# Attention, dense layer and soft mixture of experts on one core: output stores of two column parts on the copying engine's queue, with a new order and new engines

## The chip, the cores and the metric

The kernel runs on one core of a Trainium2 chip. The core has TensorE (PE; its weight loads are listed as PEld), VectorE (DVE), ScalarE (ACT), GpSimd (POOL) and SyncE (SP), each with its own queue of instructions that it works off in order. Transfers run on 16 DMA engines; an instruction on one of the engines' queues, mostly SP's, starts each of them. The metric is the device time of one execution in microseconds (us).

## The reference

```python
def reference(**kwargs):          # B, H, S, D = 4, 8, 576, 64
    attn_out = _attn_ref(...)     # rotary embedding of q and k, softmax(q k^T / 8) v
    x = attn_out.transpose(0, 2, 1, 3).reshape(B * S, H * D)   # 2304 tokens x 512
    h = x @ w_in                  # 512 -> 2048
    x = (np.maximum(h, 0) + alpha * np.minimum(h, 0)) @ w_out  # 2048 -> 512
    logits = x @ phi              # 8 experts of 4 slots: 32 columns
    d = softmax over the tokens of logits; slot_input = d.T @ x          # 32 x 512
    for e in range(8):            # 512 -> 1024 -> 512 for its 4 slots
        slot_out[e] = np.maximum(slot_input[e] @ w1[e], 0) @ w2[e]
    c = softmax over the slots of logits
    return c @ slot_out           # 2304 x 512, float32
```

## The kernel before, in words

**One list of operations.** The kernel does not issue instructions as it goes. Every step is an operation (`op`) with an engine, a cost, the operations it needs and the buffers that it takes and uses. Where a step can run on several engines, `choose` reads one digit of the table `ENGINES` (794 digits) and so picks ScalarE, VectorE or GpSimd. `Plan.order` then decodes the table `ORDER`, a full sequence of all 2791 operations, and the last loop of the kernel issues them in that sequence. What stands in an engine's queue, and in which order, is thus set by the two tables alone. A transfer stands in SP's queue, unless its line names another engine.

**The front.** Per pair of heads, q and k are loaded, rotated (L338 to L449) and multiplied on TensorE to scores `st` (L480, L489 to L493). VectorE takes each row's maximum (L498), ScalarE the exponential with its row sum (L503, tile `e`), and the rows are normalised on ScalarE (L225), VectorE (L227) or GpSimd (L229, helper `times`). Batch 0's pieces are transposed on TensorE (`pt` L578, `pc` L628); those of the other batches on VectorE (L565, L598) and by way of DRAM (`sc` L607, `ET` L617, `ett` L615). L662 multiplies by the values (`pv`). `top` (L245) transposes a per-column maximum for the scales of the weights.

**The middle.** The dense layer runs block by block: `ph` (L839) is x @ w_in; the leaky step is a product `rl` on ScalarE (L850) or VectorE (L852, chosen) and a sum `g` on VectorE (L857). w_out is not applied to the tokens: it is folded with phi for the logits (L881), and the slots collect the tokens' sums in front of w_out (L1033, L1044).

**The late loads.** When the last `pv` is done, the attention's memory becomes a pool of 29 buffers (class x). From there SP loads w_out in 16 transfers of 512 KB (`wor`, L1191) and the experts' weights in 65 transfers of 256 KB to 1 MB (`xw`, L1246); the latter use, beside the x buffers, those that the dense layer gives up. Each `wor` is turned into two TensorE operands by three steps on VectorE (`wo`, L1199, L1201, L1203), behind which its buffer is free. `px` (L1308) is the slots' sums times w_out and needs all 16.

**The end.** `expert_in` (L1365 with `relu` and transposes `pth` L1391) and `expert_out` (`po`, L1426) are the experts. The output has 512 columns, worked on in three parts of 256, 128 and 128: `PARTS = ((0, 0, 256), (1, 256, 128), (1, 384, 128))`. Per part VectorE makes `mov` of `po` (L1447, L1452). `final(ph, n)` then multiplies the tokens' weights `est` by `mov` (`pf`, L1548) for the token tiles of `n`, copies the result to `ob` on VectorE (L1553) or ScalarE (L1555, chosen), and issues the store (L1563; L1566 for the tiles 16 and 17, in two halves). In the third part a store of L1563 goes out by ScalarE's queue if ScalarE made the copy; all others of L1563 by SP's.

Of the kernel before, what the change touches and what calls it, by code (L numbers as in the profile page):

```python
# [34 lines left out]
ENGINES = (  # L35
    "020000000210000102000000000010101110101000001010201010102000100200020200102011100100000110020210111020010020001000010001"
    "002000102000010200000202010000100000000200000202000000000000200012000000002020010000000202201000001001000000222100000000"
    "200000020001021000200022000200000200001120020000000200202000200002002211210010020000202000000002000201201000220020000002"
    "022000202002002000201000101010000202000010002002210011000100000200002000002002002200000110001000202202000202000012000021"
    "000020000000020000000002210201221001120100202220000000002002000120020000000200002000202000002000200001120010000000000010"  # L40
    "000021100000110000000110201001100010010010012000000010010000001111010100000010010001200010001000001000100100000011111110"
    "00002010000101000001100000100000100011000100010001000001011110100001010111"
)


ORDER = (
    "c-"
    "mc72|!J0`#;Y)cWGZxR4Nrko5qqxMZ;)O(qhfXU_P=9X8iw#7#U<4n#nTFFrPt)EG0uV(P$;4MT!&^HI=2sy|?Awd*1K7?>V<Jr`tL2@;txi_x#?K5(DHgEYJYsAJGgb2e*mT#?WavvK"
    "GJ=9$It(*c1<unEzw`5A;rh8i42aV3$)rLeC8{18NIBp{;c&fMIp3cfE~qnOFVbS~nTgjM6WUKHLrW#&%bS*UUU?0gdjm(cS<*cf=fMnpkW!w3;>VX|D~?gPKy&=kj4KGB2Z!pXZBS+N"
    "xgJo?YBv)?pHISZQVSYh-QH%k{0Vni|%^`|}>oy;6|&R<OFpW}fjdym35CKH>rQK80eR948aF<J3|Q;8`*Pbl^cih1{%i;*bhv<n1h9Q<v=NjqudO^0lS)%3~$Npx(OK>~v`7XfT9)Q4"  # L50
    "0(<{xGGrsZD-0(y3DhmgQg$V*#K9^y^;^ol*{Za&6iin%Ksm8&<AqHdgs8?cO18bQlTpOCim#W;IBg-MIfj4WoKZrLVP2@<$D0noXg#%kBZ#!7~$m%K{jyFnwVMwIkDf%3yf*^z0!Epx"
    "UCTYPMWd1tN(>+wew(y+NU8Q=MnWjd9SPx#I~K2GwsgUTm8-"
    "d)Xg<&Pw%c>g*8f76j<DBpuVKkbPSB&HvYfLv1)*9K*f}ez9pjV{c<ow&_r@{qyng&8aNixdq^C=vD?$`m4w6v@c)1d^$I6tZnkTZf44tHhxFG{`F)IyvT!<Qx|{xBz>yNse0l*(Jc0+"
    "zh$#Sv)_e<32TzqCso>f<pVLzp0i31a$0o^g{e9jKW68R&jarxpOkJkyzbo<_DxxKhQW45$?T$_$-*U15tgD8{Mlc0L5xo1@7tR!Jp7`}x8|lDN-"
    "c#6WvUC$HyXc#!?5A{i_8rXr=%gCWzoA19IxG;1UsK4)yVXliXszWzbG*N)YA2tA&kApZt2dwu;m)S(f@n6^|ifg2taDE_;R^hzF`b}8@JID<}3}r8{2ie9V$H$T?)1pNVZ?A>!DA3Uf"
# [106 lines left out]
def attn_moe_softmoe(ctx, tc, qx, kx, vx, w_in, w_out, alpha, phi, w1, w2, tab, msks, w_out_t, out):  # L162
    nc = tc.nc
# [50 lines left out]
    PE, ACT, DVE, POOL, DMA = "PE", "ACT", "DVE", "POOL", "DMA"  # L214
# [475 lines left out]
    PF = FF // NPC  # L690
# [3 lines left out]
    sw = cst.tile([128, NPC], F32, name="sw")  # L694
# [428 lines left out]
    n = 0  # L1123
# [21 lines left out]
    for b in range(B):  # L1145
        r = 64 * (b % 2)
# [173 lines left out]
    m = None  # L1320
# [204 lines left out]
    def final(ph, n):  # L1525
# [10 lines left out]
        for i, its in enumerate(pieces):  # L1536
# [135 lines left out]
```

## Time and profile before

| | us |
|---|---|
| three runs | 555.9, 558.49, 560.74 |
| median | 558.49 |
| the profiled execution | 558.93 |
| its span in the trace | 557.1 |

How to read it: the trace is of one execution, and its times count from the start of the span, so a sum of edits is made against the profiled execution. The windows cut the span into stretches; each row has start and end, length, then busy time and number of instructions of PE, PEld, DVE, ACT and POOL, the clock that TensorE was granted (1.00 is 2.4 GHz, 0.50 is 1.2 GHz), the busy share of the 16 DMA engines, and GB/s. The timeline has start, duration, engine, line, operation, output tile and inputs, shape and count; in brackets the idle time before it and what ended it. "SPq" and "ACTq" are the issuing of transfers on SP's and ScalarE's queue. A group of instructions has its line, engine, operation, tiles, shapes and count, then busy us in all and mean ns of one, then the idle time before and what ended it.

### The profile page before, as it was taken

The page shows a single profiled execution, that of the slowest core. Times are in us where ns is not written, and L with a number is a line of the kernel's source. Part 1 is how long each engine was busy: PE and PEld are TensorE (multiplying, and loading weights), DVE is VectorE, ACT ScalarE, POOL GpSimd, SP SyncE. Part 2 cuts the span into 40 slices and gives each one's busy share as a digit, 9 for nine tenths or more (in the row PEclk, how much of TensorE's full clock was granted, in tenths as well). Part 3 has the DMA queues.
Part 4 walks back from the last instruction along what each step waited for, and adds up shares of the span by engine and source line. Part 5 has one row for each costly group of instructions (what it writes and reads, how often), then busy time and mean ns, then how long its engine had stood idle before and what let it go on. Part 6 is the DMA issues. An engine that isn't in the chain of part 4 may idle for free.

```text
span 557.1 us, 14738 instructions
## 1 busy us (share of the span) xinstructions
PE 528.2 (95%) x5752; PEld 393.6 (71%) x5752; DVE 476.0 (85%) x1092; ACT 332.6 (60%) x805; POOL 270.8 (49%) x259
## 2 busy tenths in 40 slices
PE   2899999999999998999999999999999999999994
PEld 1454566678878787787877688877778878854573
DVE  4998999999999998999999889999876999863641
ACT  3799999997778675597666477884531122330141
POOL 2474776488898876689584588642000000001000
PEclk9998999999999999999999999999999999999997
DMA  8982855918899998898987789798774999899989
GB/s 300 392 310 92 308 162 156 294 57 281 271 355 300 309 298 274 255 330 268 342 305 241 263 307 342 258 310 308 242 238 146 412 406 396 289 366 385 405 296 271
DMA packets 80805, 160.74 MB, mean 289 GB/s; under 512 B 5344, under 2 KB 44640, under 8 KB 80736
## 3 DMA queue, kind: packets, MB, share of 16 engines
q1 hardware_dynamic: 79792, 159.18, 82.7%
q8 instruction: 45, 0.74, 0.5%
q10 hardware_dynamic: 944, 0.62, 0.4%
q14 instruction: 24, 0.20, 0.1%
HBM read 115.75 MB, written 36.96 MB: 274 GB/s over the span
## 4 chain that ended last, share of the span: by engine, by line
PE 82%; DMA 8%; DVE 6%; ACT 2%; issue 1%; SPq 1%; POOL 0%; DVEq 0%
PE ph L839 33%; PE pv L662 14%; PE st L493 9%; PE pu L1033 3%; PE lg L881 3%; PE st L480 3%; PE po L1426 2%; PE pt L578 2%; DMA wraw<-in_moe_w_in_dram 2%; DMA xw<-in_moe_w_dram 2%; DMA ET<-sc 2%; PE ph L1365 2%; PE pf L1548 1%; PE st L489 1%; DVE mm L498 1%; PE st L491 1%
## 5 line engine op out<-in xcount | busy, mean ns | idle before, releaser
L839 PE MATMUL ph<-xt,w 128*128 128x256 f16 x1536 | 182.6, 273 | 0.0
L839 PEld LDWEIGHTS <-w 128*128 128x128 f16 x1728 | 162.3, 98 | 28.8 <-issue 6.5
L503 ACT ACTIVATE e<-st,mm 128x576 f32<-128x576 f32 x144 | 106.2, 738 | 47.2 <-DVE mm L498 41.1
L498 DVE TENSOR_REDUCE mm<-st 128x1 f32<-128x576 f32 x144 | 105.9, 742 | 8.0 <-PE st L493 5.0
L229 POOL TENSOR_SCALAR e<-e,mm 128x576 f32<-128x576 f32 (+1 forms) x76 | 59.4, 787 | 72.3 <-DVE mm L529 65.4
L372 POOL TENSOR_TENSOR xn<-xn,tabs 128x576 f32<-128x576 f32 x52 | 78.6, 1525 | 11.5 <-issue 5.5
L850 ACT ACTIVATE rl<-ph 128x256 f32<-128x256 f32 x105 | 38.8, 378 | 69.4 <-PE ph L839 66.7
L662 PE MATMUL pv<-ET,vt 128*64 128x256 f32 (+1 forms) x640 | 77.0, 385 | 1.7 <-DMA ET<-sc 1.5
L565 DVE STREAM_TRANSPOSE tb<-e 128x512 f32<-128x512 f32 (+1 forms) x108 | 75.7, 706 | 2.4 <-POOL e L229 1.2
L493 PE MATMUL st<-ks,qs 128*128 128x288 f32 x384 | 73.6, 315 | 0.5 <-issue 0.5
L857 DVE SCALAR_TENSOR_TENSOR g<-rl,oma,ph 128x256 f32<-128x256 f32 x144 | 66.2, 466 | 8.6 <-ACT rl L850 7.5
L662 PEld LDWEIGHTS pv<-ET,vt 128*64 128x64 f32 (+1 forms) x640 | 42.8, 137 | 28.0 <-issue 7.4
L493 PEld LDWEIGHTS st<-ks,qs 128*128 128x128 f32 x384 | 54.3, 189 | 4.9 <-issue 2.6
L225 ACT ACTIVATE e<-e,mm 128x576 f32<-128x576 f32 (+1 forms) x72 | 51.6, 723 | 7.5 <-DVE mm L529 7.0
L873 DVE STREAM_TRANSPOSE gb<-g 128x512 f32<-128x512 f32 x64 | 43.5, 690 | 0.2
L397 POOL TENSOR_TENSOR qs<-xn,qs 64x576 fp32r<-64x576 f32 x23 | 33.8, 1468 | 15.4 <-ACT qs L219 13.0
L480 PE MATMUL st<-ks 64*128 64x288 f32 (+1 forms) x168 | 30.8, 468 | 10.2 <-DVE ks L343 7.2
L375 POOL TENSOR_TENSOR xn<-xn 128x576 f32<-128x576 f32 x24 | 35.4, 1477 | 7.4 <-DVE xn L372 6.2
L480 PEld LDWEIGHTS st<-ks 64*128 64x128 f32 (+1 forms) x168 | 17.5, 195 | 19.4 <-DVE ks L343 7.2
L503 ACT ACTIVATION_READ_ACCUMULATOR e<-st,mm 128x1 f32 x144 | 28.3, 197 | 0.0
L229 POOL TENSOR_SCALAR edt<-edt,vb 128x256 f32<-128x256 f32 x5 | 2.4, 478 | 48.0 <-ACT edt L979 47.9
L578 PE MATMUL pt<-idf,e 128*128 128x128 f32 x144 | 23.4, 292 | 2.3 <-ACT e L225 1.0
(198 smaller groups left out, 805.9 us busy)
## 6 DMA issues: line engine op xcount, KB each, us to landing
sc<-tb SPq DMA_DIRECT2D x48, 576.0 KB, 4.8
ET<-sc SPq DMA_DIRECT2D x24, 1152.0 KB, 7.6
xw<-in_moe_w_dram SPq DMA_DIRECT2D x42, 512.0 KB, 8.9
xn<-in_k_dram SPq DMA_DIRECT2D x15, 576.0 KB, 6.3
xn<-in_q_dram SPq DMA_DIRECT2D x15, 576.0 KB, 5.1
wraw<-in_moe_w_in_dram SPq DMA_DIRECT2D x8, 1024.0 KB, 9.9
wraw<-in_w_out_t_dram SPq DMA_DIRECT2D x8, 1024.0 KB, 5.3
wor<-in_moe_w_out_dram SPq DMA_DIRECT2D x16, 512.0 KB, 9.5
```

Of the source, the lines that this page charges most:

```text
L225: nc.scalar.activation(dst, src, AF.Copy, scale=scale)
L229: nc.gpsimd.tensor_scalar(dst, src, scale, 1.0, ALU.mult, ALU.mult)
L372: engines[on].tensor_tensor(e["x"][:, w], e["x"][:, w], tabs[:, w], ALU.mult)
L480: nc.tensor.matmul(st[to, j, at:at + w], x, k[rows, z:z + w], start=True, stop=True)
L493: nc.tensor.matmul(st[:, j, 0:288], r["q"][:, 768 * h + 128 * s:768 * h + 128 * s + 128].bitcast(F32R), r["k"][:, a, h, ks].bitcast(F32R), ...
L498: nc.vector.tensor_reduce(c["mm"][:, h:h + 1], c["st", h][:, :, 0:288], axis=AX.XY, op=ALU.max, negate=True)
L503: nc.scalar.activation(c["e"][:, h].rearrange("p (a n) -> p a n", a=2), c["st", h][:, :, 0:288], AF.Exp, bias=c["mm"][:, h:h + 1], accum_o ...
L565: nc.vector.transpose(out=to if tail else to[:, :, 0:8].rearrange("p q (m h) j -> p q m h j", h=2)[:, :, :, h], in_=e.rearrange("p (m q j) ...
L662: nc.tensor.matmul(pv[r], v[k, 4 * h + i if i < 4 else 8 + (h if b else 0)], x, start=(i == 0), stop=(i == 4))
L839: nc.tensor.matmul(ph, wi[j][:, wp, kc, 128 * fo:128 * fo + 128], xt[:, xp, kc, :], start=(n == 0), stop=(n == 3 * KC - 1),)
L857: nc.vector.scalar_tensor_tensor(blk["g", j][:, fo, :], c["r"], oma[:, f:f + 1], c["ph"], ALU.mult, ALU.add)
L873: nc.vector.transpose(out=blk["gt", j // 2][:, f % 8 - 1:f % 8 + 1, :].rearrange("p c n -> p (c n)"), in_=blk["g", j][:, fo - 1:fo + 1, :] ...
```

## The change

One line of code says which queue a store of L1563 uses: ScalarE's, if ScalarE made the copy, now in the second and third part. The tables `ENGINES` and `ORDER` are new. Of the 794 digits 250 differ; the counts of the three digits go from 547, 134 and 113 to 563, 113 and 118. The digits behind the normalisation of `e` move 24 from ScalarE to GpSimd, 23 back, 8 from VectorE to GpSimd and 4 in other ways; those behind `rl` move 33 from VectorE to ScalarE and 21 back. In the order an operation's place moves by 9 in the median. `ORDER` has one line more, so the changed kernel's lines are one higher behind it.

```diff
 ENGINES = (
-    "020000000210000102000000000010101110101000001010201010102000100200020200102011100100000110020210111020010020001000010001"
+    "000000000200020002000000101010101010101000000010000000202000000200021201112001111010000010020201111020110120001000010001"
...
             def store(hh, i=i, its=its, on=on):
                 k = len(its)
-                queue = nc.scalar if on == ACT and ph == 2 else nc.sync
+                queue = nc.scalar if on == ACT and ph > 0 else nc.sync
                 ob = c["ob", i].rearrange("p (k d) -> p k d", k=k)
                 if len(n) == 4:
                     to = S * (n[0] // 4) + 128 * per * i
                     queue.dma_start(out[to:to + 128 * k, cols].rearrange("(r p) d -> p r d", r=k), ob)
                     return
```

The end of ScalarE's queue, from the last turned weights `est` on; `ob` is a piece of the output, and a store of 128x4x128 is one of the second or third part, one of 64x2x128 half of the tiles 16 and 17. Before:

```order
L219 ACTIVATE est<-pe 128x384 x4
L1555 ACTIVATE ob<-pf 128x512 x4
L219 ACTIVATE est<-pe 128x384
L1555 ACTIVATE ob<-pf 128x512 x5
L1555 ACTIVATE ob<-pf 128x256
L1566 DMA out_dram<-ob 64x2x128
L1555 ACTIVATE ob<-pf 128x512
L1563 DMA out_dram<-ob 128x4x128
```

After:

```order
L220 ACTIVATE est<-pe 128x384 x2
L1556 ACTIVATE ob<-pf 128x512 x2
L1556 ACTIVATE ob<-pf 128x256
L1564 DMA out_dram<-ob 128x4x128
L1556 ACTIVATE ob<-pf 128x512 x3
L1564 DMA out_dram<-ob 128x4x128 x2
L1556 ACTIVATE ob<-pf 128x512 x2
L1567 DMA out_dram<-ob 64x2x128
L1564 DMA out_dram<-ob 128x4x128 x2
```

Four stores more stand on ScalarE, and SP's stores at the end become 16 of 20. The copy of tiles 16 and 17 in the third part is VectorE's now, and ScalarE copies more of the pieces of four.

The front of TensorE's queue: `st` scores, `pt` and `pc` transposes of the exponentials, `top` that of a maximum, `rest` the first of the weights' products. Before:

```order
L480 MATMUL st<-ks 128x288 x8
L578 MATMUL pt<-idf,e 128x128 x4
L245 MATMUL top<-idf,mws 128x128
L628 MATMUL pc<-idf,e 128x128
L480 MATMUL st<-ks 128x288 x4
L578 MATMUL pt<-idf,e 128x128 x4
L285 MATMUL rest<-w_173,dg 128x512
```

After:

```order
L481 MATMUL st<-ks 128x288 x8
L246 MATMUL top<-idf,mws 128x128
L579 MATMUL pt<-idf,e 128x128 x4
L629 MATMUL pc<-idf,e 128x128
L579 MATMUL pt<-idf,e 128x128 x4
L481 MATMUL st<-ks 128x288 x4
L286 MATMUL rest<-w_172,dg 128x512
```

`top` goes ahead of the first transposes, and the second transposes ahead of the third scores.

SP's queue where the late loads begin: `wor` is w_out, `xw` experts' weights, 128x1024 is 512 KB. Before:

```order
L1191 DMA wor<-in_moe_w_out_dram 128x1024 x10
L1246 DMA xw<-in_moe_w_dram 128x1024 x2
L1191 DMA wor<-in_moe_w_out_dram 128x1024
L1246 DMA xw<-in_moe_w_dram 128x1024 x2
L1191 DMA wor<-in_moe_w_out_dram 128x1024 x2
L1246 DMA xw<-in_moe_w_dram 128x1024
L1246 DMA xw<-in_moe_w_dram 128x512
L1246 DMA xw<-in_moe_w_dram 128x1024 x3
L1191 DMA wor<-in_moe_w_out_dram 128x1024 x2
L1246 DMA xw<-in_moe_w_dram 128x512
L1246 DMA xw<-in_moe_w_dram 128x1024
L1191 DMA wor<-in_moe_w_out_dram 128x1024
```

After:

```order
L1247 DMA xw<-in_moe_w_dram 128x512
L1192 DMA wor<-in_moe_w_out_dram 128x1024 x10
L1247 DMA xw<-in_moe_w_dram 128x512
L1192 DMA wor<-in_moe_w_out_dram 128x1024
L253 DMA msk<-in_masks_dram 128x1
L1192 DMA wor<-in_moe_w_out_dram 128x1024
L1247 DMA xw<-in_moe_w_dram 128x1024
L1192 DMA wor<-in_moe_w_out_dram 128x1024 x3
L1247 DMA xw<-in_moe_w_dram 128x1024 x14
L1192 DMA wor<-in_moe_w_out_dram 128x1024
L1247 DMA xw<-in_moe_w_dram 128x1024 x2
```

The eleventh to fifteenth load of w_out stand further ahead, and the sixteenth behind fourteen loads of experts' weights that follow on each other.

## Rows read from the trace of the kernel before

**Rows 1.** Head of the page.

```profile
span 557.1 us, 14738 instructions
```

**Rows 2.** Windows by stage: busy PE, PEld, DVE, ACT, POOL; clock; DMA share; GB/s.

```profile
0.00:50.00 50.00, 35.22 (x165) 20.06 (x165) 40.93 (x83) 35.59 (x77) 26.43 (x29) 0.97 0.82 299
50.00:110.00 60.00, 58.62 (x472) 36.13 (x470) 56.75 (x107) 57.46 (x134) 36.75 (x27) 1.00 0.65 209
110.00:425.00 315.00, 312.11 (x3554) 249.90 (x3557) 290.95 (x681) 211.31 (x525) 204.49 (x198) 1.00 0.83 274
425.00:500.00 75.00, 74.54 (x900) 58.58 (x888) 63.70 (x142) 18.30 (x52) 1.20 (x4) 1.00 0.96 369
500.00:550.00 50.00, 47.72 (x676) 28.92 (x676) 23.14 (x82) 9.95 (x21) 1.90 (x2) 1.00 0.96 352
550.00:557.10 7.10, 0.00 (x0) 0.00 (x0) 0.55 (x1) 0.00 (x0) 0.00 (x0) 0.51 0.84 228
```

**Rows 3.** Timeline of the end: issues of SP and ACT, and the last copies.

```profile
540.38 3.75 SPq L1563 DMA_DIRECT2D out_dram<-ob  x5
...
548.46 2.09 DVE L1553 COPY ob<-pf 128x512 f32<-128x512 f32 x3 [1.04 <-PE pf L1548]
548.50 0.70 ACTq L1566 DMA_DIRECT2D out_dram<-ob  x1
...
551.35 2.10 SPq L1563 DMA_DIRECT2D out_dram<-ob  x2
```

**Rows 4.** Windows of the end, columns as in rows 2.

```profile
536.00:540.00 4.00, 4.00 (x77) 3.06 (x78) 1.51 (x3) 2.25 (x5) 0.00 (x0) 1.00 0.61 174
...
552.00:556.00 4.00, 0.00 (x0) 0.00 (x0) 0.00 (x0) 0.00 (x0) 0.00 (x0) 0.50 0.97 264
```

**Rows 5.** Windows of the front, columns as in rows 2.

```profile
42.00:44.00 2.00, 0.93 (x7) 0.69 (x6) 2.00 (x6) 1.76 (x4) 1.01 (x1) 1.00 0.48 180
44.00:46.00 2.00, 1.75 (x8) 1.38 (x9) 1.97 (x9) 1.94 (x5) 0.79 (x1) 0.76 0.00 0
46.00:48.00 2.00, 2.00 (x9) 1.21 (x6) 1.69 (x6) 1.87 (x5) 1.65 (x2) 0.50 0.12 14
```

**Rows 6.** Timeline of PE in the front: scores of L480.

```profile
7.17 1.33 PE L480 MATMUL st<-ks 64*128 64x288 f32 x4 [7.17 <-DVE ks L343]
...
39.49 1.24 PE L480 MATMUL st<-ks 64*128 64x288 f32 x8
...
44.51 2.61 PE L480 MATMUL st<-ks 64*128 64x288 f32 x8
```

**Rows 7.** Windows of the late loads, columns as in rows 2.

```profile
468.00:472.00 4.00, 4.00 (x39) 3.13 (x40) 3.90 (x11) 1.81 (x5) 0.00 (x0) 1.00 1.03 410
472.00:476.00 4.00, 4.00 (x39) 3.65 (x37) 2.41 (x7) 2.36 (x7) 0.62 (x3) 1.00 0.49 173
476.00:480.00 4.00, 4.00 (x147) 2.70 (x149) 3.88 (x9) 0.52 (x2) 0.09 (x1) 1.00 0.85 267
480.00:484.00 4.00, 4.00 (x43) 3.33 (x34) 3.93 (x8) 1.84 (x5) 0.00 (x0) 1.00 0.95 322
```

**Rows 8.** Waits of SP, 424 to 545 us: in total, times, longest.

```profile
SPq L1246 <- DVE wo L1199: 9.6, 2, 8.4
```

**Rows 9.** Timeline of PE, 524 to 526 us.

```profile
524.82 0.41 PE L1426 MATMUL po<-xw,hz 128*32 128x128 f32 x2 [0.31 <-DMA xw<-in_moe_w_dram]
```

**Rows 10.** Groups of instructions by line and shape.

```profile
L229 POOL TENSOR_SCALAR e<-e,mm 128x576 f32<-128x576 f32 x68 | 55.6, 822 | 70.1 <-DVE mm L529 63.4 <-ACT mm L524 5.2
...
L850 ACT ACTIVATE rl<-ph 128x256 f32<-128x256 f32 x105 | 38.8, 378 | 69.4 <-PE ph L839 66.7 <-DVE g L857 1.9 <-DVE mm L498 0.6
...
L852 DVE TENSOR_SCALAR rl<-ph 128x256 f32<-128x256 f32 x39 | 16.0, 409 | 4.2 <-PE ph L839 3.9 <-issue 0.2
...
L1201 DVE SCALAR_TENSOR_TENSOR wo<-wor,wo 128x512 int32<-128x512 int32 x16 | 10.9, 683 | 0.0
...
L227 DVE TENSOR_SCALAR e<-e,mm 128x576 f32<-128x576 f32 x12 | 5.9, 500 | 0.1
```

More of the change, by code (lines that the diff above doesn't have):

```diff
@@ new lines @@
+    "200210220200001000002220000202000200110021201001000200222000002000002211200200020000200220000200001210000020200100000002"
+    "222000000000000200201200021001202022010002012200200000200000000000122000002000002000200110100000000002000200002200210210"
+    "000020000202020000002000200010200201120000202220000002000012000000221001000202022000200000002000000200100100000000000000"
+    "000020100000001000010000110111000000001000010100000000000000010120100000100100000001200001000010011011002100101001000000"
@@ L51 @@
[L51 to L55, printed above, removed]
@@ new lines @@
+    "Zo{xx=9a@wv)2<&kvv>@lye2ev0%8ovFfEn$bc!pMQ)<oWsV{rH6mSI#mp_ti}IbRET((-0CrQUBUBCQ-"
+    "XR*F_by<ife&&LnrO>}sXH!{2inAi2;3$cwrPtALmDM=Uaz7cR{l`@~wF(YP?Z%_%8oXGgy%C*KkWXnt=$C=PZlZ&+@0y-XG0A7Nsl>)U*LoAZc_!9mB&MkXCOJVdwEchxHT^xjwJ-AX"
+    "+!1=gF?w7>AB${86sfVvZU7fcR)^XG|MhLqEbQ`6f9*2o!?&Y)syD>Z&Y-qv01_N&jlBCl*euC%p}w=dqa3X&Fb(tK`^4317Ub;+w7NGY2uV!5yiic4D}Z_#}@6iTh^Ak#G@e9x)Gp-Q"
+    "kwqg|gEzXV@M@+r+fwY5B;bMaMv<rb_zb2Ni(N`!r1ZTvJd1!i1Wa&E}>y{BI5ZulkT?qoO?cM~e}r%nHJ`Gzl+Ntj?0yBw{eIeA~^%t+l9?cFYqsac)40OkYiH>>8(swF#HA^LLE)cZ"
@@ new lines @@
+    "8!>-g`6m9RCU!h9S=!m}i9t53=jyP0FA-5%p3gUx$m7lu6^p)GmQVRn3;V^reF>)-"
+    "hO4)E07jMi&7xU<~z2WW!h#1ayWZ=YD110`p+mmXP7%HA6*4#8^I$M=@$?zz9c?H7vGi<|4>Ns(0achW-<aAzu=>>H^a=1$%TKT3>>dfBm!ggw?Jl?kh^J>8mm!!-"
+    "D$^z8DF*Ef6J58h#)W*im03KHugwE@15TR;ygiT9^t-@^~;Yvc>31$!(@H#6Y<FPNP;bBmil>ksRj+twB5G*7zcEon6DP<{8E^Ka`D=0BVgN6p;K9cb7UE&odn)!@su-"
+    "00tE4{kU2ZFkKaZ~X6hwpYRZ<%V2`{Vg!*@KVVq&;z6RnG}7~vUF3(>Ae%+48Wd<Ls`WT7;702AG^>o&OB}&oic5QYk2Un+tYF#SDZ|iHpp-"
+    "KcjS-$2w|`&YG=!Il?-O)I;{QnjSL1mJOGd2aC-NOFYW$&S$^~qDgS#hT}St?Yl4&@84%U_dgW;WHEnW>_vaq}Hc)kRO}WyT+_$aNv^r)-"
@@ new lines @@
+    "H&A3tYpV_=(_v5ShTAq#XIC6gwWqpC%XIhU9lI=YbXN^nJL!#u_QLhf?}l}9T4dm*&KG}r`N=X%N#fojoly(s4T|{}P{T;>X=_ys?29C?<PUqIAfGMEb^J5r1?BvQiP;ykQZlsZwQyh7"
+    "A<G(9VhwGC^26iFgwoyD0~`;-"
+    "NWFcxocz`V|4{06B?27%ZWx{2zwrh9H8o73QtSv*?DBm0@aoDF=dTX18Uy5<m_jEqYfxRp|IR(Fo#SbAFJ`%Qs6ur(dh~S1z^!ktM2vevQg(Z_x_oxHW{!#sy7*YK?xCLyHr-"
+    "4<yzajdFn0SqC_J*!JmRp0@9JMU3PvR#k%#>LGb>@)-P;ZnnCH1{f^NyhvJJ+K7gEo31;$-"
+    "?w`ty*329KXaM`0@zb%j5wm@eyxz;^s?c~`M*{H|fm{%V;<?=b{WlwU~p{`A?t${xts80k1c$y@8-}LGCadKGd;mw}GO^IJMdb(KI0L-"
@@ new lines @@
+    "ho1VOS7k9=F2b+m8!CQehrL5nF;{h0E><rdLD0r+1uGziYi0Y@mZk~(hD$sg=b7UlZ^0nuZIg57@rX4%hv9SthiSM%YW)I6`aeQfT!d#07K;SfJ^#?#XIL`sGtJmuTOPtdyl)z>F2;hZ"
+    "a(3OcRcd6j03Ro3n0c3R{+-Bx4m=d;x%$u@Rv`YmjO4QIV=g?iSTl6OY@F_G{6-CEt&-{44*+Q3M0Wdx~3ydEmAH6$!w`!3y5Hl)J-"
+    ";%tETUJr5rhFj%o*=oHZZM)u#gm!uC$YC9_OxHG@Z~jo}#4LW&_1;#t|A$}B0(9oWli{8K4<;r982s)UnlVbACUN;#sG1TOn>Hb_KQJDksAa*Vjg(*3`_E{v`=QUB_fMG`PI-"
+    "X~mC02PGR^jX%ECZfRA=7kzAd#R9hB*0m(~}`#}ok7DR0;50_~6e)KE9jv`7cKh5<a&eHNAnH9$eum(QIgtVGfYWVf<Q-"
@@ new lines @@
+    "p=1`NSfsC(6q}_2HK}ULVwBhvmtbub~Zf`9{Lv<JQ|<$$xlfGL#yHMNeRPkFV)O8BSFGkTFgjVwW*u*V5syevW=VAzexX6OSQE<6&oP!F1NXB81FyePFXm`KC3K-jd$IkFnui0L-"
+    "dl%R`L1G$z68b##7pz<e_Ex;ZE7trlCJbz^u{$zVAE+G@P8ucWzbe?A{q!0pzs}@69Q?i;@;wPB?Y&H*(`9m16N<%YPyJZPM}EUJWM`vbUYs-Ld8Of~5NGaw<Pcw$+-EM-"
+    "*JrB0E8{5>9nXyR|qHDE|bue)oYEy;_-"
+    "WKpeDn$h0iWKrNvXd}!#>QYXxXXyET_3_P5et6N|wB~SW!aCEwM!z7B;Rt5$*RJwFI=>4Hy)O2@*!n~rXWWo)f0Zskj!Xh9~hWyXZ==|a=E$6J<(F#==34?(FSr<r^!?JDpYXTp2k`F+"
+    "7x_0-51E6+uuZM8}p>yIL!41;g!Fo-=B!EJ@G?N;L3Fgs7kR8M$3LtAK->ZM^S$WIvdWO4?A$(*L0Y<rJJsEZA;%m^Vr?lGTX8Ny(XWQwv<d1^~Ul;(?Neb-xXAYO}w=y??szDzOQpaR"
@@ new lines @@
+    "FnSg?!$wHe}-"
+    "LB5~xg5#RvaSSz;CjCt|K$Jh5AFen$63_ogb9`)8L`cYqXL2uNI2*j)clGB7%v!UZ1D$J^smA4O+X|p`bF+UE|w6r@sp^7%m}1VG$RN>1pgpe><IA)s#t;t10p4`Jift`AYW(_1<49J1"
+    "TUx$gvLD!m;xE1CW|RSWCbJ$GyxLWD?g4siy$#=7>j7ITg=Y!n?%enKicOZ2E}5R*uRhsJlkskcv2&kLk$##00l7+0yJp8D<+lDcpx|iQwr<Jl08lQhtozNB7#A=6KT;b-"
+    "Hjg{|I4vbqEkwA3k!&t8G^*FNHk5*oxn=FQHw((YHZFCoqU@^1j0T+G~L*{fCPR*(2Q8=ZuB829)X)&H_kOpAS};AsPSgteG$@b4B<cx1S7?E2*;2J-"
+    ">uo(1oDQnMhnug5DvRS_5=<M<v_GS<Z6!M#~2bD5J-"
+    "w3ffZ>uOoIrpE@VJ(6hWXNgr~$L5j}e!wQxo#Y#;zIgyJ=*HSY<|8l~pv)p(8<q9zDDqDEsBRwhznGCotBumN~m1VT}OV2E+}7ZV_I6q;K2aD)aWylo;7ad2v^Q^+CeVk5x=mV<!=){T"
@@ new lines @@
+    "3d7!A&nV2WQrF$266smA%iF(3<G7$+#?9q>$4&sQym%OG0hM0132XqF!()#weTM6i$wjK@Q~H%yEtNVM;<c8YIsLXJgCVX=kCa3-"
+    ")$0^1AAsTOC2r4Y^!4zG>yPiRt1sBy$3g5nG^B*qA~!Xbm(oVdk!v3O-UAzIW&9RkHnF#<?P2Z_0P^++Ozm2zTg7-4Zyl)NE-%=17bfj_sgABrO|E#F00be!X-"
+    "xMBDeVbHR$ta#q?0pT3+ICS!p4Ccj6LJgRM#1Mf+C;|A46O`jLAZKdvMMp4n(umIa4kHu>N>m~Y2|zJ&!8sp>;2z5tvP|M=5K^p5L=T!FIrO@UEshgd(dx4(9Atu8oG1?0o}N96%#bG#"
+    "tVqErhrQx32`rQUU@|;NvYe)V;t}2>!H8fX*@8g4CV=IVxbzSx3LZh>#S$Ny@bH}Imc(m;ULtWsbCw`NLO9;V)Zqew0pe=oXpviVmJ_{4Js+V^zJ*K)DL`d}!zz&+Au!&7uuoBg09Nn}"
```

53 lines of the change are left out of this document (11 added, 42 removed).

## The prediction

> **What bounds the kernel now.** I read the head of the page first, then the busy times by stage, then the timeline of the end, the front and the late loads. The span is 557.1 us [rows 1]; the profiled execution took 558.93, so 1.83 us lie outside the span. The median of the three runs is 558.49, which is 0.44 below the profiled execution.
>
> The stages show where TensorE stands idle [rows 2]. In 0 to 50 us it is busy for 35.22, so 14.78 are idle; 7.17 of these lie before the first matmul [rows 6] and 7.61 behind it. From 50 to 550 us the idle times are 1.38, 2.89, 0.46 and 2.28, together 7.0 us in 500. Then come 7.1 us in which only stores run. All in all 28.9 of 557.1 us are idle: the kernel is bound by TensorE in the middle, by input and rope at the front, and by the output stores at the end. The change keeps TensorE's matmuls and only sorts them, so whatever it gains has to come out of these 28.9 us, and whatever it costs has to show as new idle time or as a lower clock.
>
> **Stores on ScalarE's queue.** This is the one edited line. In the new order four stores leave SP (20 become 16) and go to ScalarE. The end of the old kernel: SP issues from 540.38 on, the last batch begins at 551.35 and is through at 553.45, and the last byte lands 3.65 us later [rows 3]. These are 16 issues in 13.07 us, 0.82 us each; four fewer free 3.3 us of SP's time. Is it SP's time that ends the kernel? The DMA engines are at 0.97 in 552 to 556 but at 0.61 in 536 to 540 [rows 4]. So the transfers are full at the end, and all that an earlier issue can use is the idle share before, 0.39 x 4 = 1.56 us. That is the best end of this term. The copies that feed the last stores run on VectorE from 548.46 to 550.55 [rows 3], and no queue lets a store leave before its copy, so I take a quarter: -0.4 us. The other end: ScalarE pays up to 0.70 us an issue [rows 3], and in its new queue three stores stand ahead of its last two copies, among them one of the second part. Were all three in the way, those copies and their stores would come 3 x 0.70 = 2.1 us later. Term: -0.4, bounds -1.6 and +2.1.
>
> The last stretches show full DMA engines whichever queue issued [rows 4]. The Trainium skill's "DMA: Bandwidth & Descriptors", section "Issuing engines are not separate DMA queues", says that transfers started by ScalarE, SyncE or GpSimd end on the same 16 DMA engines, and that spreading the starts only saves the time that a sequencer takes to start them. By that rule the term is 0, not -0.4, and the trace agrees as far as 0.97 goes; the 0.61 just before speaks for a small gain.
>
> **The front.** The new order puts the transpose of a maximum (`top`) first and both transposes of the first pieces ahead of the next scores, where four scores stood between them before. The matmuls are the same. What can change is how long TensorE waits and which clock it gets. After a stretch in which it was busy for 0.93 of 2 us, the granted clock falls to a mean of 0.76 in 44 to 46 and stands at 0.50, the 1.2 GHz level, in 46 to 48 [rows 5]. Eight scores that take 1.24 us at 39.49 take 2.61 at 44.51 [rows 6]. The windows give the price: 2 x 0.24 + 2 x 0.50 = 1.5 us. The new order may avoid this dip or have another: bounds -1.5 and +1.5, and with nothing in the order that decides it, 0.
>
> The trace has one dip behind gaps, in rows 5. The Trainium skill's "TensorE: Matmul & The Clock Gate", section "HAM oscillation — how this bites in real kernels", describes a kernel that falls to the lower clock again at each wait for data. By that rule a second gap of that kind would cost another 1.5 us and no gap would give 1.5 back; the one dip in the trace agrees and says nothing on which it will be.
>
> **The late loads.** Behind the attention's last matmuls SP sends 16 loads of w_out and 65 of the experts' weights. Both begin with ten of w_out (the new order with half an expert load ahead). Then the old one sends the other six among eleven expert loads, the last behind all eleven; the new one sends five of them behind two expert loads and the sixteenth behind fourteen more in a row. The bytes are the same. TensorE works through here (0.46 us idle in 75 [rows 2]), so the order costs something only if bytes come late behind 500 us. SP's queue runs in order, and a load stands until its buffer is free: the longest such wait is 8.4 us, on the conversion of w_out on VectorE [rows 8]. In that hole the rates fall to 173, 267 and 322 GB/s against 410 before it [rows 7], a loss of (237 + 143 + 88) x 4 / 410 = 4.6 us of transfer. At the end of it all TensorE waited for expert weights for 0.31 us [rows 9]. So the old order has no margin: a longer loss goes to the end, one for one, but a shorter one gives back no more than these 0.31. In the new order SP will stand at other places, and by the order of the releases I expect about as much lost. Term 0, bounds -0.3 and +4.6 (the hole twice).
>
> **The engines.** 250 of 794 choices differ, most of them swaps. Net, GpSimd gets seven more normalisations of 0.822 us, 5.8 us in all [rows 10]; it is busy for 267.67 of the first 425 us [rows 2], 63%, so there is room. Twelve of the half-leaky steps go from VectorE (0.409 each) to ScalarE (0.378): 4.9 us less there, 4.5 more here [rows 10]. VectorE is the fuller one, 290.95 of 315 in the main stage, where ScalarE has 211.31 [rows 2]. This is the right way round, but TensorE waits only 2.89 us in this stage, so the gain is at most that, and it is hidden unless a chain runs late. If the cover fails, a normalisation on GpSimd is 0.32 us longer than the 0.50 that VectorE needs [rows 10]; seven in the path would be 2.3 us. Term 0, bounds -2.9 and +2.3.
>
> **The sum.** 558.93 - 0.4 + 0 + 0 + 0 = 558.5 for an execution like the profiled one. Less the 0.44 by which that lies above the median: 558.1 us.
>
> **Rivals.**
> A, the forecast: all is absorbed but some tenths at the end.
> B, the loads come late (slower). The place is SP's queue in 445 to 500. The sixteenth w_out load stands behind fourteen expert loads, 14 x 0.524 MB = 7.3 MB, or 18 us at 410 GB/s; those need buffers that the conversions on VectorE release, which is busy for 63.70 of 75 us there [rows 2], and what SP waits for at one load holds all behind it. For it: the 8.4 us and the missing margin. Against it: the ten first loads are unchanged, and five more follow sooner. It decides as soon as SP loses more than the old 4.6 us. With one such hole more, 4.6, and the two long steps of the last conversion in the path, 2 x 0.683 = 1.4 [rows 10]: 558.1 + 6.0 = 564.1.
> C, the front closes up (faster). No dip, -1.5; half of the 7.61 us behind the first matmul gone, -3.8; and the full 1.56 at the end instead of 0.4, -1.2. 558.1 - 6.5 = 551.6. For it: the front is the one place with idle time to win. Against it: the front waits for rope and its inputs, with VectorE at 40.93 and ScalarE at 35.59 of 50 [rows 2], and the new order puts no less on them.
> D, the queue buys nothing and ScalarE's issues hold its copies up: +0.4 + 2.1, so 560.6. For it: DMA at 0.97. Against it: the last part has two copies on VectorE, which go on meanwhile.
>
> **How the numbers follow.** A 0.48, B 0.15, C 0.15, D 0.22. About 1% (5.6 us) is what a measurement of this kernel can tell from no change, so faster means under 552.9 and slower over 564.1. Faster: 0.11 of C's 0.15 and 0.04 of A, by the spread of the three runs: 0.15. Slower: 0.10 of B, and 0.04 of D and A: 0.14. The rest, 0.71, is the same. The range goes from 552.0 to 565.0: it holds A and D whole, half of C and half of B, and so leaves some 0.16 out. A's own range is 555 to 561.
>
> **What would show it.** Right: last issue of the stores at 552 to 553.5, DMA still over 0.95 behind 550; idle time of TensorE in 50 to 550 at 6 to 9 us; the rate behind 500 us with no new wait on expert weights over 1 us; idle behind the first matmul 6 to 9 us. B is shown by waits of TensorE for expert weights of several us between 505 and 545, with longer or more stands of SP before. C is shown by under 5 us idle in the front and no stretch at 0.50. D is shown by ScalarE's last copies beginning over 1 us later behind its own issues. A clock under 0.98 over the span, or several us of new idle time in 110 to 425, would be none of these and make the forecast wrong.

## The result, and the profile after

The changed kernel takes 561.58 us (median of 20 runs, 558.45 to 565.43) where the kernel before takes 557.93 beside it (20 runs, 553.97 to 563.49). The ratio is 1.0059, 95% interval 1.0040 to 1.0078: 0.6% slower, some 3.3 us. 558.1 was forecast, with a small gain; the time lies in the range and the direction is wrong.

The profiled execution of the changed kernel is one of its faster ones: 559.30 us, span 557.4. The windows by stage, as in [rows 2]:

```profile
0.00:50.00 50.00, 35.44 (x180) 20.33 (x181) 42.10 (x87) 37.74 (x84) 25.45 (x28) 1.00 0.82 293
50.00:110.00 60.00, 59.20 (x483) 37.10 (x482) 57.87 (x111) 57.41 (x133) 33.84 (x27) 1.00 0.72 229
110.00:425.00 315.00, 309.17 (x3518) 247.74 (x3517) 288.24 (x665) 203.23 (x514) 212.24 (x211) 1.00 0.81 271
425.00:500.00 75.00, 74.68 (x908) 58.73 (x903) 60.81 (x133) 22.18 (x60) 1.93 (x4) 1.00 0.96 363
500.00:550.00 50.00, 46.63 (x678) 27.95 (x676) 24.30 (x82) 10.31 (x21) 1.90 (x2) 1.00 0.98 360
550.00:557.40 7.40, 0.00 (x0) 0.00 (x0) 0.00 (x0) 0.17 (x1) 0.00 (x0) 0.52 0.82 232
```

TensorE's idle time by stage goes from 14.78, 1.38, 2.89, 0.46, 2.28 and 7.1 us to 14.56, 0.80, 5.83, 0.32, 3.37 and 7.4. The new idle time is in 110 to 425 us, 2.9 us more. (Of the 1.1 us more in 500 to 550, 0.56 is only that TensorE ends earlier there, at 549.21 against 549.77. The old profile holds a stretch at half clock [rows 5], priced at 1.5 us, and the new one none; that is one reason why the two spans nearly agree.) The two longest waits of TensorE in 110 to 425 us, in total, times, longest:

```profile
PE ph L840 <- DVE g L858: 2.7, 1, 2.7
PE pv L663 <- DMA ET<-sc: 1.7, 1, 1.7
```

A wait of the second kind stood before too, at another place (1.5 us, at 211 us); the first is new. On the timeline of TensorE they are

```profile
138.93 1.47 PE L840 MATMUL ph<-xt,w 128*128 128x256 f16 x12 [2.67 <-DVE g L858]
...
182.24 2.38 PE L663 MATMUL pv<-ET,vt 128*64 128x256 f32 x20 [1.74 <-DMA ET<-sc]
```

What VectorE's `g` waited for is found by going from engine to engine. VectorE stands 3.49 us in front of a transpose `tb`, and behind that transpose `g` stands in its queue:

```profile
137.14 0.71 DVE L566 STREAM_TRANSPOSE tb<-e 128x512 f32<-128x512 f32 x1 [3.49 <-POOL e L230]
```

The transpose waits for a normalisation `e` on GpSimd (136.36), and GpSimd had itself stood 3.54 us in front of a rope step, for a load of q:

```profile
117.83 0.75 POOL L230 TENSOR_SCALAR e<-e,mm 128x576 f32<-128x576 f32 x1
118.67 1.42 POOL L398 TENSOR_TENSOR qs<-xn,qs 64x576 fp32r<-64x576 f32 x1
120.04 1.38 POOL L222 CAST ks<-xn 64x576 fp32r<-64x576 f32 x2
121.52 2.31 POOL L230 TENSOR_SCALAR e<-e,mm 128x576 f32<-128x576 f32 x2
123.81 3.78 POOL L373 TENSOR_TENSOR xn<-xn,tabs 128x576 f32<-128x576 f32 x2
127.66 2.27 POOL L398 TENSOR_TENSOR qs<-xn,qs 64x576 fp32r<-64x576 f32 x1
130.02 1.43 POOL L376 TENSOR_TENSOR xn<-xn 128x576 f32<-128x576 f32 x1
134.98 1.40 POOL L373 TENSOR_TENSOR xn<-xn,tabs 128x576 f32<-128x576 f32 x1 [3.54 <-DMA xn<-in_q_dram]
```

The load came late because SP had stood 11 us at it, for the `qs` of L398 on GpSimd, the last user of the input's buffer (waits of SP, 100 to 135 us, then its timeline):

```profile
SPq L370 <- POOL qs L398: 15.0, 2, 11.0
```

```profile
129.97 0.33 SPq L370 DMA_DIRECT2D xn<-in_q_dram  x1
```

In the kernel before the same load went out at 126.61:

```profile
126.61 0.34 SPq L369 DMA_DIRECT2D xn<-in_q_dram  x1
```

So GpSimd works without a pause from 111.46 to 131.45 us (shown above from 117.83 on), its rope steps end late, the buffer comes free late, and the load is 3.4 us late. In the kernel before GpSimd had such a stretch too, but from 116.33 to 129.08. The windows of the two, first before, then after (the fifth pair of numbers is GpSimd's):

```profile
116.33:129.08 12.75, 12.75 (x115) 10.13 (x114) 12.45 (x28) 12.26 (x28) 12.35 (x9) 1.00 0.44 133
111.46:131.45 19.99, 19.91 (x184) 16.36 (x183) 19.92 (x43) 17.92 (x46) 19.42 (x15) 1.00 0.17 35
```

Which of the instructions on GpSimd are new there? Five choices of 105 to 125 us went from ScalarE to GpSimd: three normalisations, one copy of keys (`ks`) and one of queries (`qs`). The expectations below call both copies those of keys; choice 236 is the one of queries.

### The profile page after: what moved, and what is told of

Its sections match the earlier page's. It is cut to its first block, busy times and chain, and to the rows that moved or that the text cites. A ratio compares the mean times of both kernels' runs of the same rounds, so it can differ in the third digit from the quotient of the medians.

```text
span 557.4 us, 14749 instructions
## 1 busy us (share of the span) xinstructions
PE 525.1 (94%) x5752; PEld 391.9 (70%) x5752; DVE 473.3 (85%) x1075; ACT 331.1 (59%) x811; POOL 275.4 (49%) x270
## 4 chain that ended last, share of the span: by engine, by line
PE 69%; DVE 9%; DMA 6%; ACT 6%; POOL 4%; issue 2%; SPq 1%; ACTq 0%; POOLq 0%; DVEq 0%
PE ph L840 27%; PE pv L663 12%; PE st L494 6%; PE pu L1034 4%; PE lg L882 3%; PE po L1427 3%; DMA sc<-tb 3%; PE ph L1366 3%; PE st L481 2%; DVE mm L499 2%; PE pt L579 2%; DMA ET<-sc 2%; DMA wraw<-in_moe_w_in_dram 1%; ACT e L504 1%; DVE tb L566 1%
## 5 line engine op out<-in xcount | busy, mean ns | idle before, releaser
L230 POOL TENSOR_SCALAR e<-e,mm 128x576 f32<-128x576 f32 (+1 forms) x85 | 66.5, 788 | 73.1 <-DVE mm L530 58.7
L851 ACT ACTIVATE rl<-ph 128x256 f32<-128x256 f32 x117 | 43.5, 379 | 62.4 <-PE ph L840 59.5
L226 ACT ACTIVATE e<-e,mm 128x576 f32<-128x576 f32 (+1 forms) x69 | 50.3, 737 | 6.1 <-DVE mm L530 5.8
L398 POOL TENSOR_TENSOR qs<-xn,qs 64x576 fp32r<-64x576 f32 x24 | 34.9, 1456 | 8.9 <-ACT qs L220 7.1
L481 PE MATMUL st<-ks 64*128 64x288 f32 (+1 forms) x168 | 29.6, 453 | 9.4 <-DVE ks L344 7.5
L376 POOL TENSOR_TENSOR xn<-xn 128x576 f32<-128x576 f32 x22 | 31.1, 1414 | 2.9 <-DVE xn L373 2.2
```

Of the source, the lines that this page charges most:

```text
L226: nc.scalar.activation(dst, src, AF.Copy, scale=scale)
L230: nc.gpsimd.tensor_scalar(dst, src, scale, 1.0, ALU.mult, ALU.mult)
L481: nc.tensor.matmul(st[to, j, at:at + w], x, k[rows, z:z + w], start=True, stop=True)
```

## The experiments

The first theory: the loss is this one stall in the middle, made by the tables. Rival 1: it is ScalarE's issues at the end. Rival 2: clock lost in the front and the late part. Rival 3: the late loads or the end. Every kernel was compared with runs of the kernel before on its own chip. The names "old" and "new" in the edits stand for the two kernels' lists of operations, in order; an engine goes with its operation.

**The queue line alone, and all but the queue line.** Two edits to the same line, on the kernel before and on the changed one:

```diff
-                queue = nc.scalar if on == ACT and ph == 2 else nc.sync
+                queue = nc.scalar if on == ACT and ph > 0 else nc.sync
```

> The kernel before with the one code line of the change alone: stores of the second and third part leave by the queue of the copying engine, tables of before. Theory (the loss is a stall in the middle of the new order): the queue line is worth nothing by itself, within 0.5 us of the kernel before. Rival 1 (the loss comes from ScalarE's issues at the end): 1 to 3 us slower than before, with ScalarE's last copies later behind its own issues.

Ratio to the kernel before 0.9975 (0.9943 to 1.0006).

> The kernel before with the queue line alone, the kernel of the first experiment once more, for a narrower interval. Theory: 0.5 to 1.5 us faster than before, from issues at the end that are through earlier. Rival (the first run's lead was chance): within 0.5 us of the kernel before.

Ratio 1.0005 (0.9982 to 1.0028). The first lead did not come again, and both intervals hold 1: the line is worth nothing that these runs can measure.

> The changed kernel with the old code line: new tables, but the stores of the second part all leave by SP's queue. Theory: as slow as the changed kernel, some 3 us over the kernel before. Rival 1: the loss goes and it is level with the kernel before.

Ratio 1.0054 (1.0022 to 1.0086): as slow as the changed kernel. Rival 1 is out; the loss comes with the tables.

**The late part alone.**

```diff
-order = old
+first = set(new[:2248])
+order = [o for o in old if o in first] + new[2248:]
```

> Order and engines of before up to the point where the attention's memory is given up (the first 425 us), order, engines and queue line of the changed kernel from there. Theory: the late part costs at most 1 us, so within 1 us of the kernel before. Rival 3 (the late loads or the end are what is slower): 2 to 4 us over the kernel before, with longer waits of TensorE behind 500 us than the kernel before's 2.3 us.

Ratio 0.9995 (0.9963 to 1.0028). New late loads, new end and new queue line together cost nothing that shows (up to 1.6 us isn't excluded). Most of the loss lies in the first 425 us.

**The one stall.** One operation of the new order moved, so that GpSimd's queue has

```diff
-L373 TENSOR_TENSOR xn<-xn,tabs 128x576
-L230 TENSOR_SCALAR e<-e,mm 128x576 x2
-L373 TENSOR_TENSOR xn<-xn,tabs 128x576
+L230 TENSOR_SCALAR e<-e,mm 128x576 x2
+L373 TENSOR_TENSOR xn<-xn,tabs 128x576 x2
```

> The changed kernel with one operation moved: on GpSimd two normalisations stand ahead of the rope step that waits 3.5 us for its q load at 131 us, instead of behind it. Theory: VectorE's wait for GpSimd of 3.5 us and TensorE's wait of 2.7 us for g at 136 us go, and the time falls by 2 to 3 us against the changed kernel, to within 1 us of the kernel before. Rival 2 (the loss is clock lost in the front and the late part): the wait goes too, but the time stays 2 to 4 us over the kernel before.

Ratio 1.0071 (1.0039 to 1.0103): a miss. The wait for `g` shrank, to 1.52 us, but the one for ET grew from 1.74 to 3.30:

```profile
138.61 1.47 PE L840 MATMUL ph<-xt,w 128*128 128x256 f16 x12 [1.52 <-DVE g L858]
...
183.65 3.90 PE L663 MATMUL pv<-ET,vt 128*64 128x256 f32 x20 [3.30 <-DMA ET<-sc]
```

The stall is a place where lateness shows, and not its source: with the rope steps as late as before, the lateness came out at the next place.

**Where in the first 425 us.** Three seams and one stretch by itself:

```diff
-order = new
+first = set(new[:K])                 # K = 500, 1050 or 1150
+order = [o for o in old if o in first] + new[K:]
```

> Order and engines of before for the first 500 operations (about 105 us), those of the changed kernel behind them. Theory 2: the loss lies behind, so within 1 us of the changed kernel. Rival 4 (the loss comes from the front, above all from clock lost there): level with the kernel before.

K = 500: ratio 1.0095 (1.0058 to 1.0131). The old front doesn't mend it, and rival 4 is out. The time is in the middle 2 us above that of the changed kernel, where theory 2 had at most 1; the two intervals overlap.

> Order and engines of before for the first 1050 operations (about 195 us), those of the changed kernel behind them. Theory 2: the loss is gone, within 1.5 us of the kernel before, mean clock about 0.993. Rival 5 (the loss lies between 195 and 425 us): 2 to 4 us over the kernel before.

K = 1050: ratio 1.0038 (1.0009 to 1.0068). That is 2.1 us over the kernel before, within rival 5's range and not within theory 2's; the interval overlaps that of the changed kernel. A wait of 1.83 us stands right at the seam, so the seam was moved.

> As the kernel with before's first 1050 operations, but with the seam 100 operations later, at about 215 us: order and engines of before for 1150 operations, those of the changed kernel behind. Theory 2 (the loss lies in 105 to 195 us; the 0.4% left with the first seam comes from TensorE's wait of 1.8 us at that seam): within 1 us of the kernel before, no wait of over 1 us at 194 us. Rival 5 (part of the loss lies between 215 and 425 us): still 1.5 to 3 us over the kernel before.

K = 1150: ratio 1.0023 (0.9993 to 1.0053). The wait at 194 us is gone, and the interval holds 1: nothing behind 215 us is shown to cost time, and some tenths of a per cent aren't excluded (the 1.3 us lie between the two expectations).

```diff
-order = old
+x = [o for o in old if o in set(new[:500])] + new[500:1050]
+order = x + [o for o in old if o not in set(x)]
```

> The kernel before with order and engines of the changed kernel between operations 500 and 1050 (about 105 to 195 us) alone, old queue line. Theory 2: as slow as the changed kernel, 2.5 to 4 us over the kernel before, mean clock about 0.990, with TensorE's waits for g and for ET. Rivals 4 and 5: level with the kernel before.

Ratio 1.0123 (1.0076 to 1.0171): the new stretch of 105 to 195 us alone makes the old kernel slower, by 6.9 us in the middle. That is more than theory 2 forecast and more than the whole change costs; that a seam at each end adds to it is likely, but no run shows it. Rivals 4 and 5 forecast level.

**The front and the queue, without that stretch.** The counterpart: new operations to 500, old ones behind, and the new queue line.

```diff
-order = old
+first = set(old[:500])
+order = [o for o in new if o in first] + old[500:]
```

> Order and engines of the changed kernel for the first 500 operations (about 105 us) and its queue line, order and engines of before behind. Theory 2 (the new front gains some 2 us, the queue line about 1, and only the stretch behind 105 us loses): 2 to 4 us faster than the kernel before. Rival 4 (the front gains nothing): level with the kernel before to 1 us faster.

Ratio 1.0014 (0.9985 to 1.0044): level, and the 2 to 4 us of theory 2 did not come. The new front gains nothing that shows, as rival 4 had it; no kernel tried beats the one before by more than the noise. With this and the late part alone, rivals 2 and 3 are out as well.

**Engines or order.** First the five choices given back in the changed kernel:

```diff
-ENGINES: 207, 209, 210 (norm), 227 (copy of keys), 236 (copy of queries) = GpSimd
+ENGINES: 207, 209, 210 (norm), 227 (copy of keys), 236 (copy of queries) = ScalarE
```

> The changed kernel with five choices of 107 to 125 us given back from GpSimd to ScalarE as before (three normalisations and two copies of keys, some 4.4 us of GpSimd), order unchanged. Theory 2 (GpSimd is overloaded there: its late rope steps keep the input buffers, so the q load comes late and TensorE waits twice, at 136 and at 181 us, each wait now and then followed by a stretch at half clock): the q load is issued some 4 us earlier, TensorE's waits in 110 to 200 us fall from 4.4 us to under 2.2, the time falls by 2 to 4 us against the changed kernel, mean granted clock back to 0.993. Rival (VectorE and the stores of the transposed pieces set the fetch of ET at 181 us whatever GpSimd does): the wait at 181 us stays or grows, and the time stays 2 to 4 us over the kernel before.

Ratio 1.0036 (1.0002 to 1.0070). These links did what the theory said of them: the load of q goes out 5.6 us earlier than at 129.97, the wait at 136 us is gone, 0.28 us is left of the one at 181, and the mean clock is 0.9932 (0.9935 for the kernel before beside it).

```profile
124.36 0.33 SPq L370 DMA_DIRECT2D xn<-in_q_dram  x1
```

But ScalarE now has the work in its own queue, in front of an exponential, and TensorE waits for that:

```profile
121.16 0.79 PE L494 MATMUL st<-ks,qs 128*128 128x288 f32 x4 [1.80 <-ACT e L504]
```

TensorE's idle time in 100 to 200 us falls only from 4.71 to 3.81 us, and the time by 1.3 us where 2 to 4 were forecast, which the overlap of the two intervals leaves unproven. So this is half of a confirmation. The same five on the kernel before, the other way round:

```diff
-ENGINES: 207, 209, 210 (norm), 227 (copy of keys), 236 (copy of queries) = ScalarE
+ENGINES: 207, 209, 210 (norm), 227 (copy of keys), 236 (copy of queries) = GpSimd
```

> The kernel before with five choices given from ScalarE to GpSimd as in the changed kernel (three normalisations and two copies of keys at 107 to 125 us), order, queue line and all else of before. Theory 2 (it is GpSimd's load there): 1.5 to 4 us slower than before, with a wait of TensorE of over 1 us between 120 and 200 us that before has not, and GpSimd's rope steps of 120 us some 4 us later. Rival 6 (it is the order, not the engines): within 1 us of the kernel before.

Ratio 1.0062 (1.0034 to 1.0089). Five digits of 794, on an engine that is busy for half of the span, cost the kernel before as much as the whole change did. The way there is shorter than theory 2 had it. The load of q goes out at 127.39, 0.8 us later than before the change (2.4 us, if one counts the 1.6 us by which TensorE is ahead at 105 us in this profile) and not 4, and no step on GpSimd waits for a load there. A transpose on VectorE stands 2.74 us for a normalisation on GpSimd, `g` stands behind the transpose, and TensorE behind `g`; two shorter waits follow (0.61 and 0.55 us):

```profile
127.39 0.34 SPq L369 DMA_DIRECT2D xn<-in_q_dram  x1
124.42 1.47 POOL L229 TENSOR_SCALAR e<-e,mm 128x576 f32<-128x576 f32 x2
125.91 0.71 DVE L565 STREAM_TRANSPOSE tb<-e 128x512 f32<-128x512 f32 x1 [2.74 <-POOL e L229]
127.14 0.63 PE L578 MATMUL pt<-idf,e 128*128 128x128 f32 x4 [1.15 <-DVE g L857]
```

So the link from the normalisation to TensorE stands in both kernels, and the one by way of the buffer and the load in the changed kernel alone.

> The kernel before with three of the five choices alone: the three normalisations go from ScalarE to GpSimd, the two copies of keys stay on ScalarE. Theory 2: most of the loss of the five, 1.5 to 3 us over the kernel before, with 1.5 to 2.5 us more idle time of TensorE in 100 to 150 us than the 0.64 us of before. Rival 7 (the key copies, which stand ahead of the rope's end, make the loss): within 1 us of the kernel before.

(The same without 227 and 236.) Ratio 1.0021 (0.9987 to 1.0055): neither time is excluded. With three moved, TensorE's idle time in 100 to 150 us rises by 1.05 us, less than half of the 2.43 that five bring, and less than the 1.5 to 2.5 of theory 2.

> The changed kernel with the engines of before for its operations 500 to 1050 (about 105 to 195 us, 55 choices), in the order of the changed kernel. Theory 2: the waits at 136 and 181 us go and the time comes down to within 1.5 us of the kernel before. Rival 6 (the order alone delays the stretch): it stays 2 to 5 us over the kernel before.

```diff
-ENGINES of new[500:1050]: 55 digits of the changed kernel
+ENGINES of new[500:1050]: the digits of before
```

Ratio 1.0152 (1.0129 to 1.0176), the slowest of all. So it isn't the engines alone either: the new order with the old engines is worse than with its own, and worse than rival 6 had it. The load of q goes out at 121.67 here, 8.3 us earlier than in the changed kernel, so a late load isn't what makes this kernel slow. TensorE waits for exponentials on ScalarE (3.1 us in four waits) and once for a rope step on GpSimd:

```profile
121.67 0.33 SPq L370 DMA_DIRECT2D xn<-in_q_dram  x1
180.38 1.15 PE L494 MATMUL st<-ks,qs 128*128 128x288 f32 x4 [2.19 <-POOL qs L398]
```

Order and engines of this stretch fit each other or they don't.

**All kernels in one table.** One window follows the loss from profile to profile: TensorE's busy time in 100 to 200 us. Four of the rows, in their order the kernel before, the changed one, the old order with five choices moved, the new order with the old engines (columns as in [rows 2]):

```profile
100.00:200.00 100.00, 99.36 (x1010) 79.47 (x1009) 95.64 (x213) 80.58 (x196) 83.19 (x76) 1.00 0.81 267
```

```profile
100.00:200.00 100.00, 95.29 (x973) 76.04 (x971) 92.03 (x202) 74.37 (x186) 81.95 (x77) 1.00 0.77 259
```

```profile
100.00:200.00 100.00, 96.93 (x985) 76.80 (x982) 93.60 (x206) 74.02 (x185) 83.94 (x79) 1.00 0.78 259
```

```profile
100.00:200.00 100.00, 93.00 (x919) 72.68 (x913) 87.99 (x193) 71.15 (x176) 76.23 (x73) 0.98 0.75 247
```

| kernel | idle of TensorE in 100 to 200, us | ratio |
|---|---|---|
| before | 0.64 | 1 |
| queue line alone (both runs) | 0.64, 0.72 | 0.9975, 1.0005 |
| late part alone | 0.65 | 0.9995 |
| before to 215 us | 0.64 | 1.0023 |
| front and queue line | 1.39 | 1.0014 |
| three normalisations moved | 1.97 | 1.0021 |
| before to 195 us | 2.47 | 1.0038 |
| five choices moved | 3.07 | 1.0062 |
| changed kernel, old queue line | 3.67 | 1.0054 |
| changed kernel, five given back | 3.81 | 1.0036 |
| changed kernel | 4.71 | 1.0059 |
| changed kernel, front of before | 5.30 | 1.0095 |
| changed kernel, normalisations first | 5.57 | 1.0071 |
| before, new stretch alone | 6.69 | 1.0123 |
| changed kernel, engines of before in the stretch | 7.00 | 1.0152 |

A straight line through the sixteen points (1% is 5.58 us) has a slope of 1.1 us of time for each us of idle time here, with a correlation of 0.94. One profile stands for each kernel, so single points are rough; the line is what counts. Whether it is steeper than one to one can't be told: by the scatter of the points the slope is uncertain by 0.1 to 0.2 (an estimate).

## Why the prediction was wrong

**The engines: this step failed.** It said that GpSimd "is busy for 267.67 of the first 425 us [rows 2], 63%, so there is room", and put seven normalisations at a term of 0 with an upper end of +2.3. Two things were wrong in it. The share is an average over 425 us. In 100 to 200 us GpSimd was busy for 83.19 of 100 before the change, and from 116.33 to 129.08 us it had no pause at all. And the price was that of the moved instructions themselves (0.32 us each, seven net), where the price is paid by what stands behind them: in the old kernel with the five choices a transpose on VectorE behind the late normalisation, `g`, and TensorE; in the changed kernel also a rope step that frees an input buffer, a load that waits for the buffer, and a normalisation behind the next rope step. Netting 24 normalisations one way against 23 the other hid that three of them fall into 20 us, and the copies of the rope, two of which fall there too, weren't counted. These five cost 3.5 us in the old kernel (0.62%, by its interval 1.9 to 5.0), in the middle more than the upper end given for all 250.

**The order in the middle** had no term at all, and no reason was given for that. The stretch of 105 to 195 us in its new order, with its engines, cost the old kernel 1.23%, and the new order with the old engines there cost 1.52%, against 0.62% for the five choices.

**The middle stage's reserve** was read rightly but used wrongly. TensorE had only 2.89 us idle in 110 to 425 us [rows 2], and I took that as a limit on the gain. It says nothing about the loss, which has no such limit: in 100 to 200 us TensorE was idle for 0.64 us, VectorE busy for 95.64 and ScalarE for 80.58, so a new order had nearly nothing to win here and much to lose.

**Stores on ScalarE's queue: -0.4 was forecast;** the two runs give -0.25% and +0.05%, which is no gain that can be told, and the interval of the second excludes more than 1 us. The rule that was weighed against this term, in the Trainium skill's "DMA: Bandwidth & Descriptors", section "Issuing engines are not separate DMA queues", gave 0, which is within what these runs measure, as is -0.4. In the profile of the first queue run SP's last issue is through 2.95 us behind TensorE's last product (548.95 to 551.90), against 3.68 before (549.77 to 553.45): the sequencer's time is saved there, and the times show nothing of it. In the changed kernel ScalarE's last two issues take over as the latest, through at 552.51:

```profile
549.97 1.81 SPq L1564 DMA_DIRECT2D out_dram<-ob  x2
550.58 1.93 ACTq L1564 DMA_DIRECT2D out_dram<-ob  x2
```

**The front: 0 was forecast.** With the new front and the new queue line the old kernel stays level (1.0014), so right. The dip at 44 us [rows 5, 6] doesn't belong to every execution with the old front: the clock falls there in three of the ten profiles with that front, and in none of the six with the new one, which is too few to tell the two apart.

**The late loads: 0 was forecast,** and rival B did not come. The late part alone is level. The hole of [rows 7] is mostly gone in the changed kernel, where the same stretch reads

```profile
472.00:476.00 4.00, 4.00 (x39) 3.61 (x38) 2.70 (x7) 2.10 (x8) 0.92 (x2) 1.00 0.93 314
476.00:480.00 4.00, 4.00 (x146) 2.75 (x149) 3.88 (x9) 1.58 (x4) 0.52 (x2) 1.00 0.94 337
480.00:484.00 4.00, 4.00 (x60) 3.33 (x34) 4.00 (x10) 1.69 (x4) 0.00 (x0) 1.00 0.96 335
```

It brought nothing, as the wait of 0.31 us [rows 9] had said.

**The chances.** Slower was expected only from the loads and the tail. The list of rivals had no entry for a helper engine in the middle, although the prediction itself named that sign ("several us of new idle time in 110 to 425") as one that no case would explain. That 561.58 lies in the range of 552.0 to 565.0 is luck: the upper part of the range was there for B and D, the loads and ScalarE's issues, and neither is what cost the time.

What stays open: which part of the new order, beside the five choices, delays the stretch, and how much of the changed kernel's own loss the five choices are; the kernels show that order and engines act together and no single edit was found that gives the time back. The 0.2% that the kernel with the old first 215 us keeps is not told from nothing.

## What to carry to other kernels

Before an engine's idle share is called room, look at it in the stretch where the work is added, and ask what stands behind that work in the queue: the price of a moved instruction can be the delay of everything behind it, down to the buffer and the load that its last user frees. Count moves by place, not net. And a stall seen in a trace is not yet a cause: take it away, and if the next one grows, the lateness comes from further up.

## What the runs showed of the hardware

Behind a wait of TensorE in the middle the clock fell in some executions. In the changed kernel with the old queue line the wait for `g` was 2.16 us, and behind it the granted clock went down to 0.50, the 1.2 GHz level:

```profile
136.00:138.00 2.00, 0.91 (x9) 0.78 (x8) 0.73 (x2) 0.00 (x0) 2.00 (x4) 1.00 0.98 323
138.00:140.00 2.00, 0.94 (x6) 0.67 (x6) 2.00 (x5) 1.34 (x5) 1.92 (x2) 0.80 0.87 296
140.00:142.00 2.00, 2.00 (x11) 1.63 (x10) 1.70 (x5) 0.82 (x3) 2.00 (x2) 0.50 0.98 289
142.00:144.00 2.00, 2.00 (x27) 0.93 (x26) 1.87 (x5) 1.29 (x6) 1.94 (x4) 0.84 1.03 347
```

That is 2 x (0.20 + 0.50 + 0.16) = 1.7 us on top of 2.16 (after the wait of 3.30 us in the kernel with the normalisations first it fell in the same way). In the profile of the changed kernel itself a longer wait at the same place, 2.67 us, was followed by 1.00 throughout. Up to the stores the two kernels are the same program, so it pays this in some executions and not in others. Nor does all of it reach the end. Here are both waits of the profile with the fall:

```profile
139.06 2.62 PE L840 MATMUL ph<-xt,w 128*128 128x256 f16 x12 [2.16 <-DVE g L858]
182.48 2.38 PE L663 MATMUL pv<-ET,vt 128*64 128x256 f32 x20 [1.25 <-DMA ET<-sc]
```

The profile without it has them end at 138.93 and 182.24. So the fall's 1.7 us have shrunk to about 0.1 at the second wait, which is 0.5 us shorter.

Over the runs the mean granted clock is 0.9904 for the changed kernel (20 runs) and 0.9931 for the one before (35 runs beside the first experiments). If all of it reached the end, 0.0027 of 560 us would be 1.5 us, close to half of the loss, and among the 20 runs those with the lower clock are the longer ones (correlation 0.83). But the kernel before with the five choices moved lost its 0.62% at a mean clock of 0.9946, against 0.9938 beside it. So how much of the loss is the clock's isn't shown. The Trainium skill's "TensorE: Matmul & The Clock Gate", section "HAM oscillation — how this bites in real kernels", tells of a kernel with such a fall at each wait for data; here it follows some waits and not others.

The granted clock isn't the whole of TensorE's speed at the start. Eight scores at 12.80 us took 2.91 us in the kernel before, about as long as at half clock (2.61 in [rows 6]), while the granted clock of the window from 12 to 14 us reads 1.00:

```profile
12.80 2.91 PE L480 MATMUL st<-ks 64*128 64x288 f32 x8 [1.95 <-ACT e L503]
```

At 26.97 us eight of the same form take 1.24. The Trainium skill's "TensorE: Matmul & The Clock Gate", section "Part 1: The HAM clock gate (the "warmup" mystery)", says that TensorE begins at the lower clock; the 2.91 us agree, the window's 1.00 does not, and no run shows why. So the clock column is to be read with the time of one instruction beside it.
